# Seven half-width block products for the first feed-forward product of the last batch

## The chip, the cores and the metric

The kernel is one program on one core of a Trainium2 chip. The metric is the device time of one execution in microseconds (us), the median of a few runs. The program before has a median of 403.88 us in 3 runs (403.68 to 404.29).

## What is computed

For 8 batches of 448 tokens and 12 heads of 64 elements, attention with normalised queries and keys, and then two products with an activation between them:

```python
q_n = q / (norm(q) + 1e-06);  k_n = k / (norm(k) + 1e-06)
attn = softmax(q_n @ k_n.T / tau)            # per batch and head
x = (attn @ v), heads side by side           # 3584 x 768
h = x @ w_in                                 # 768 x 2048
g = h * clip(h + 3, 0, 6) / 6
out = g @ w_out                              # 2048 x 768
```

Inputs and output are float32 in memory; the kernel works with bf16 operands and float32 sums.

## The kernel before

The attention of a batch is six **pairs of heads**, 48 pairs in all, numbered `i`. A loop over `i` (from 18 on; the pairs before stand in a hand-written list, `PLAN`) issues one pair at a time: scores, exponentials on ACT, products with V, the loads and the normalisation for pairs to come, and between these some **units** of the two products of batches that are done. The order of each engine's queue is the order in which the program issues the work; there is no scheduler. Engines run their queues in order and wait on each other through semaphores.

A unit of the **first product** (`mm1_unit`, line 574) takes one of 16 blocks of 128 columns of `w_in` (index `fc`) over all 448 tokens of a batch. It is six matmuls with 448 moving columns, one for each block of 128 rows of `w_in`. ACT then makes `u = relu(h/6 + 1/2)` (line 589), and DVE `g = min(u, 1) * h` in bf16 (line 595). The result for the last batch goes to `g_last`, a part of the buffer `big`, whose loads have ended by then; for the others it goes to `gT0` or `gT1`.

The **second product** (`product_unit`, line 734) already works by seven block products in place of eight. Token blocks of 128 are taken in pairs (numbered 0 to 10 here), and each pair is a 2 x 2 block product in seven parts named "1" to "7". Each part is eight matmuls with 384 moving columns (line 753). "4.8" is part 4 of pair 8. Parts 3 and 4 take plain blocks, the others sums of two blocks. Those sums are made by DVE from bf16 blocks (`g_sum`, line 713, the operation at line 731), 128x1024 elements each. ACT copies some parts out (lines 772, 801), POOL adds copies in three operations (lines 782, 783, 786), and DVE adds the rest (lines 778, 810). A token block without a partner is a `single_unit` (line 824, "s6.0" for batch 6), 16 matmuls and a copy by DVE (line 843).

After the loop comes a **last stage**, `units[NP]` (lines 903 to 912): two units of the first product of batch 6, all 16 of batch 7, pairs 7 and 8 and the single block of batch 6, and then pairs 9 and 10, which need the whole first product of batch 7. Each unit's work on ACT, DVE and POOL is issued right behind its matmuls.

Results of matmuls lie in a ring of six PSUM banks (`M` x4, `Y`, `Z`), taken strictly in turn (`next_bank`). A unit cannot start before the bank's last reader is done. In the loop, POOL squares and normalises queries and keys (lines 229, 286), casts V (line 305) and copies small key blocks (line 392). These stop with pair 47, so POOL's last operation in the loop is the cast that starts at 322.59 us of the trace.

Of the kernel before, what the change touches and what calls it, by code (L numbers as in the profile page):

```python
# [8 lines left out]
FP32 = mybir.dt.float32  # L9
BF16 = mybir.dt.bfloat16  # L10
AF = mybir.ActivationFunctionType
ALU = mybir.AluOpType
# [47 lines left out]
]  # L60


@with_exitstack
def kernel(
# [10 lines left out]
    nc = tc.nc  # L75
    B, H, S, D = q.shape
    d_model, d_ff = moe_w_in.shape
    inv_tau = 1.0 / float(tau)

    HP = H // 2  # L80
    NP = B * HP
    CC = d_model // 128
    FCN = d_ff // 128
    MH = d_model // 2
    SM = 384
    SR = S - SM
# [7 lines left out]
    sb = ctx.enter_context(tc.tile_pool(name="sb", bufs=2))  # L94
# [28 lines left out]
    RAW, VAL, SUM = 14 * D, 20 * D, KC * 128 // 2  # L123
    big = const.tile([128, (NR + 2) * RAW + NV * VAL], FP32, name="big", tag="big")
# [20 lines left out]
    nrms = [const.tile([128, 7, 2, D], BF16, name=f"nrm{i}", tag=f"nrm{i}") for i in range(3)]  # L145
# [3 lines left out]
    bias = const.tile([128, 2], FP32, name="bias", tag="bias")  # L149
    eps_bias, half_bias = bias[:, 0:1], bias[:, 1:2]  # L150
# [402 lines left out]
    def g_of(b):  # L553
        if b == B - 1:
            needs(("NM", NP - 1), ("RE", NP - 1), ("VC", NP - 1))
            return g_last
        return gT[b % 2]
# [90 lines left out]
    def firsts(b, *fcs):  # L648
        return [(mm1_unit, b, fc) for fc in fcs]
# [13 lines left out]
    summed, g_summed, issued_products = set(), set(), set()  # L663
# [7 lines left out]
    wide = [big[:, c : c + MH] for c in range(0, 3 * MH, MH)]  # L671
    wide_late = [tail(c, MH) for c in range(TAIL, TAIL + 2 * (len(PAIRS) - LOOP) * MH, MH)]

    def sum_of(n, what):

        if what == "e":
            return gs["1"] if n < B - 2 else late_sums[1]["e"]
        if n < LOOP or n == len(PAIRS) - 1:
            return gs[what + str(n % 2) if what == "7" else what]
        return late_sums[n % 2][what]  # L680
# [143 lines left out]
    def single_unit(b, m):  # L824
# [21 lines left out]

        post["v"].append(store)

    def sums(n, names):
        return [(g_sum, n, x) for x in names]  # L850

# [3 lines left out]
    def products(text):  # L855

        u = []
        for x in text.split():
            name, n = x.split(".")
            if name[0] == "s":  # L860
                u.append((single_unit, int(name[1]), int(n)))
            else:
                u.append((product_unit, int(n), name[0], None, name[1:] == "a"))
        return u
# [9 lines left out]
    APART = {(n, y) for n in range(len(PAIRS)) for x, y in (("5a", "3"), ("2a", "4")) if f"{x}.{n}" in " ".join(TURNS.values()).split()}  # L874
    side = {
        18: [(weight_sums, "y4", KC // 2, KC // 2)], 19: sums(0, "62"), 20: sums(0, "1"),
        21: sums(1, "75"), 22: sums(1, "621"),
        25: sums(2, "75"), 26: sums(2, "62"), 27: sums(2, "1"), 28: [(g_left, 2)], 29: sums(2, "e"),
        31: sums(3, "75"), 32: sums(3, "62"), 33: sums(3, "1"),
        34: sums(4, "75"), 35: sums(4, "621"), 37: [(g_left, 4)],  # L880
        38: sums(5, "75"), 39: sums(5, "62"), 40: sums(5, "1"), 41: sums(4, "e"),
        43: sums(6, "75"), 44: sums(6, "62"), 45: sums(6, "1"), 46: sums(7, "75"), 47: sums(7, "62"),
    }
    units = {}
    carry = firsts(1, FCN - 2, FCN - 1)
    for b in range(2, B - 1):
        first = firsts(b, *range(FCN))
        for n, x in enumerate([0, 3, 3, 3, 3, 2]):
            i = (b + 1) * HP + n
            u = carry + [first.pop(0) for _ in range(x)]  # L890
            carry = []
            *p, last = products(TURNS[i])
            if i == NP - 1:
                p, last = [last], None
            x = 0 if n == 1 else 1 if n in (0, 5) and i > FIRST else 2
            units[i] = u[:x] + p + u[x:]
            units[i] += [last] if last else []
        carry = first
    units[FIRST] += sums(0, "75")

    b = B - 1
    f = firsts(b, *range(FCN))
    units[NP] = sums(7, "1") + carry[:1] + products("4.7") + carry[1:] + [(g_left, B - 2)] + products("2.7")
    units[NP] += products("3.8") + sums(8, "75") + products("1.7 4.8") + sums(8, "62") + products("6.7 5.8") + sums(8, "1")
    units[NP] += products("7.7") + sums(B - 2, "e")
    for n, x in enumerate("2176"):
        units[NP] += f[n : n + 1] + products(x + ".8")
    units[NP] += f[4:] + products(f"s{B - 2}.0") + sums(9, "75") + products(f"s{B - 2}.1") + sums(9, "62")
    units[NP] += products("3.9 4.9") + sums(9, "1") + products("5.9") + sums(10, "75") + products("2.9 3.10") + sums(10, "62")
    units[NP] += products("4.10 5.10") + sums(10, "1") + products("2.10 1.9 1.10")  # L910
    units[NP] += [(product_unit, n, x, 2) for n, x in ((9, "7"), (9, "6"), (10, "6"))]
# [38 lines left out]
    def finish_units(e):  # L950
        post[e].pop(0)()
# [15 lines left out]
    def do(op, *args):  # L967
        OPS[op](*args)
        key = (op,) + tuple(a for a in args if isinstance(a, int))
        if op not in ("RE", "NM", "LQ"):  # L970
            issued.add(key[:3] if op == "SC" else key)
# [40 lines left out]
    for i in range(FIRST, NP):  # L1012
        assert not stream
        stream = list(units[i])
        n_u = len(stream)
        even = i % 2 == 0

        def prepare(*what):
            for op, n, *args in what:
                if n < (NP // 2 if op in ("NO", "LV") else NP):  # L1020
                    do(op, n, *args)

        if i > FIRST:
# [12 lines left out]
        if (i - 1) % HP > 3:  # L1036
            do("XB", i - 1)
        elif even:
            do("XP", i - 2)
        if even:  # L1040
            prepare(("XD", i + 2))
        do("UU", 1)
        do("SC", i, 3)
        do("EX", i, 3)
        if not even:
            prepare(("CS", i + 1))
        prepare(("SQ", i + 5, "p", 0, 7))
        do("UU", 1)
        n = 2
        if i == FIRST:  # L1050
            do("RE", i + 4)
        if not even:
            prepare(("NO", (i + 3) // 2))
            if n_u > 3 and stream[0][0] is product_unit and units[i][1][0] is mm1_unit:
                do("UU", 1)
                n += 1
            prepare(("CK", i + 1), ("CK", i + 2))
        do("UU", n_u - n - 1)
        prepare(("NM", i + 3, "p"), ("VC", i + 2, "p"))
        if even:  # L1060
            prepare(("XD", i + 3))
        do("UU", 1)
        prepare(("RE", i + 5), ("LQ", i + 7))
        if not even:
            prepare(("LV", (i + 5) // 2))
        while post["p"]:
            finish_units("p")
        do("VA", i, 0)
# [42 lines left out]
```

## Time and profile before

| what | value |
|---|---|
| median of 3 runs | 403.88 us |
| lowest, highest | 403.68, 404.29 us |
| span of the profiled execution | 404.4 us |
| PE busy | 393.7 us, 97% |
| DVE busy | 288.7 us, 71% |
| ACT busy | 276.7 us, 68% |
| POOL busy | 236.7 us, 59% |
| granted TensorE clock | 1.000 |

The profiled execution has no time of its own beside its span, which is 0.5 us above the median of the runs. A span is counted from the first to the last instruction. In the views, `L580` is line 580 of the program before, `out<-in` names the tiles, and a timeline row has the start in us, the length in us, and `x6` when six instructions that follow each other are merged. A row of merged groups gives busy time and the mean length of one instruction in ns. An instruction's length contains its drain, so the pitch of matmuls in a stream is found from rows with many of them.

### The profile page before, as it was taken

What the parts mean: (1) busy time and instruction counts of PE and PEld (TensorE: products, weight loads), DVE (VectorE), ACT (ScalarE), POOL (GpSimd) and SP (SyncE); (2) the same over time, 40 slices, a digit from 0 to 9 for tenths busy, and PEclk for the clock granted to TensorE, in tenths of its full rate; (3) what the DMA queues carried; (4) which work ended last, traced back from release to release, by engine and by line L of the source; (5) the groups of instructions that cost most, each with busy time, mean ns of one, the idle gap of its engine ahead of it and who ended that gap; (6) DMA issues with size and microseconds to landing.
All of it is one profiled execution on the core that took longest, in us unless ns stands there. A gap on an engine that the chain in (4) does not pass through costs nothing.

```text
span 404.4 us, 9618 instructions
## 1 busy us (share of the span) xinstructions
PE 393.7 (97%) x3689; PEld 234.5 (58%) x3689; DVE 288.7 (71%) x512; ACT 276.7 (68%) x604; POOL 236.7 (59%) x232
## 2 busy tenths in 40 slices
PE   7798999999999999999999999999999999999996
PEld 5566656555665555655555556555565556555564
DVE  5898787878498777777857887587656666655663
ACT  4899989887377687687768768768758755225230
POOL 4799945862744997588486875876664600510070
PEclk9999999999999999999999999999999999999999
DMA  8899999999877748786779659986863523140134
GB/s 285 247 235 243 221 221 213 170 219 202 181 168 179 167 111 209 185 222 129 169 200 194 140 149 163 180 190 136 193 147 76 112 45 63 36 88 20 25 74 99
DMA packets 93166, 63.75 MB, mean 158 GB/s; under 512 B 56128, under 2 KB 93120, under 8 KB 93120
## 3 DMA queue, kind: packets, MB, share of 16 engines
q1 hardware_dynamic: 87408, 56.45, 61.1%
q0 software_dynamic: 5312, 6.29, 9.5%
q8 instruction: 29, 0.48, 0.6%
q10 hardware_dynamic: 400, 0.39, 0.3%
q14 instruction: 17, 0.14, 0.1%
HBM read 45.61 MB, written 11.01 MB: 140 GB/s over the span
## 4 chain that ended last, share of the span: by engine, by line
PE 88%; ACT 4%; DVE 3%; DMA 3%; SPq 1%; issue 0%; DVEq 0%; ACTq 0%
PE M L580 23%; PE M L753 16%; PE PV L475 11%; PE Y L580 6%; PE Z L580 6%; PE M L435 6%; PE Z L753 5%; PE Y L753 4%; PE M L833 3%; PE M L627 3%; ACT at L453 3%; DMA big<-in_q_dram 3%; PE Y L435 1%; PE Z L435 1%; PE Y L833 1%; PE Y L627 1%
## 5 line engine op out<-in xcount | busy, mean ns | idle before, releaser
L453 ACT ACTIVATE at<-M 128x448 bf16<-128x448 f32 x194 | 96.8, 564 | 23.2 <-PE M L435 20.7
L580 PEld LDWEIGHTS <-w_in_sb 128*128 128x128 bf16 x768 | 72.3, 98 | 63.1 <-issue 2.5
L580 PE MATMUL M<-xT,w_in_sb 128*128 128x448 bf16 x504 | 107.4, 352 | 0.1
L286 POOL TENSOR_TENSOR nrm<-big,r 128x896 bf16<-128x896 f32 (+1 forms) x47 | 78.1, 1665 | 14.8 <-issue 4.6
L229 POOL TENSOR_TENSOR big<-big 128x896 f32<-128x896 f32 (+5 forms) x45 | 68.1, 1519 | 14.8 <-DMA big<-in_k_dram 8.2
L589 ACT ACTIVATE u<-M,bias 128x448 bf16<-128x448 f32 x84 | 54.9, 655 | 26.3 <-PE M L580 26.0
L475 PEld LDWEIGHTS <-at 128*128 128x128 bf16 (+1 forms) x1536 | 54.1, 97 | 19.9 <-issue 12.1
L595 DVE SCALAR_TENSOR_TENSOR gT<-u,M 128x448 bf16<-128x448 bf16 x73 | 44.6, 617 | 29.2 <-ACT u L589 28.4
L475 PE MATMUL PV<-vx,at 128*128 128x65 bf16 (+1 forms) x1536 | 62.7, 194 | 0.0
L241 DVE TENSOR_REDUCE n<-big 128x14 f32<-128x896 f32 (+1 forms) x50 | 51.5, 1037 | 0.3 <-ACT big L227 0.2
L392 POOL COPY km<-tT 64x128 bf16<-64x128 bf16 x34 | 14.4, 424 | 61.9 <-PE M L435 25.9
L782 POOL TENSOR_TENSOR big<-big 128x384 f32<-128x384 f32 x11 | 11.8, 1077 | 54.6 <-ACT big L801 54.5
L753 PEld LDWEIGHTS <-gT 128*128 128x128 bf16 x288 | 27.8, 98 | 20.0 <-DVE gT L731 0.6
L753 PE MATMUL M<-w_out_sb,gT 128*128 128x384 bf16 x192 | 35.0, 326 | 0.1
L496 DVE TENSOR_TENSOR on<-PV,rc 128x512 bf16<-128x512 f32 x48 | 33.2, 691 | 1.7
L435 PE MATMUL M<-tT,kz 64*128 64x448 bf16 (+1 forms) x171 | 30.9, 351 | 0.5 <-ACT at L453 0.5
L453 ACT ACTIVATE at<-Y 128x448 bf16<-128x448 f32 x50 | 28.2, 564 | 4.3 <-PE Z L435 4.3
L753 PEld LDWEIGHTS <-gs 128*128 128x128 bf16 x224 | 21.5, 98 | 14.7 <-DVE gs L731 0.3
L453 ACT ACTIVATE at<-Z 128x448 bf16<-128x448 f32 x50 | 28.2, 565 | 2.6 <-PE M L435 2.6
L305 POOL CAST vx<-big 128x512 bf16<-128x512 f32 x39 | 28.2, 728 | 3.1 <-DMA big<-in_v_dram 3.0
L580 PE MATMUL Z<-xT,w_in_sb 128*128 128x448 bf16 x132 | 28.6, 353 | 0.0
L580 PE MATMUL Y<-xT,w_in_sb 128*128 128x448 bf16 x132 | 28.6, 352 | 0.0
(128 smaller groups left out, 574.7 us busy)
## 6 DMA issues: line engine op xcount, KB each, us to landing
big<-in_k_dram SPq DMA_DIRECT2D x24, 448.0 KB, 5.1
big<-in_q_dram SPq DMA_DIRECT2D x24, 448.0 KB, 4.5
out_dram<-o SPq DMA_DIRECT2D x107, 96.0 KB, 2.2
big<-in_v_dram SPq DMA_DIRECT2D x48, 128.0 KB, 4.7
big<-in_v_dram SPq DMA_DIRECT2D x48, 96.0 KB, 4.4
w_in_sb<-in_moe_w_in_dram POOLq DMA_DIRECT2D x8, 384.0 KB, 10.4
w_out_sb<-in_moe_w_out_dram POOLq DMA_DIRECT2D x4, 768.0 KB, 10.8
tT<-nrm SPq DMA_TRANSPOSE x34, 2.8
```

The costliest lines, as they stand in the source:

```text
L229: engines[e].tensor_tensor(out=o, in0=i, in1=i, op=ALU.mult)
L241: nc.vector.tensor_reduce(out=n2_and_r[0][:, d % 2, j % 2, c], in_=sq[:, :, :, :].rearrange("p g c d -> p (g c) d")[:, c, :], axis=AX.X, o ...
L286: engines[e].tensor_tensor(out=nrm[:, :, g, :].rearrange("p c g d -> p g c d"), in0=raw_of[j][:, g, :, :], in1=n2_and_r[4][:, d % 2, j % 2, :]
L305: (engines[e].copy if e == "a" else engines[e].tensor_copy)(out=o, in_=f)
L435: nc.tensor.matmul(o, ks, qt[rows], start=True, stop=True)
L453: nc.scalar.activation(out=o, in_=x, func=AF.Exp, scale=inv_tau)
L475: nc.tensor.matmul(pv_out(j, h), at[rows, n, q_cols(i // HP, j)], vt[rows, 3 + h if name == "M" else 5 * h + int(name[1]), :], start=(name ...
L496: nc.vector.tensor_tensor(out=on[:, :, :, :].rearrange("p j h d -> p h j d"), in0=pv4[:, :, :, 0:D], in1=rc[:, :, :].to_broadcast([128, 2, ...
L580: nc.tensor.matmul(ps[:, 0:S], w_in_sb[:, cc, fc * 128 : (fc + 1) * 128], x[:, cc, 0:S], start=(cc == 0), stop=(cc == CC - 1),)
L589: nc.scalar.activation(out=u[:, :], in_=ps[:, 0:S], func=AF.Relu, bias=half_bias, scale=1.0 / 6.0)
L595: nc.vector.scalar_tensor_tensor(out=g[:, fc, c0 : c0 + S], in0=u[:, :], scalar=1.0, in1=ps[:, 0:S], op0=ALU.min, op1=ALU.mult,)
L753: nc.tensor.matmul(m, lhs[:, c, :], rhs[:, c, c0 : c0 + width], start=(base is None and c == 0), stop=(c == KC - 1), skip_group_check=True,)
```

## The change

The first product of the last batch (batch 7) no longer runs as 16 units of six matmuls. It runs as **eight groups**, numbered `n` from 0 to 7. Group `n` makes columns blocks `n` and `n + 8` for both halves of the tokens (224 each): a 2 x 2 block product over the halves of the columns of `w_in`, the halves of its rows, and the halves of the tokens, in **seven** products of three matmuls with 224 moving columns. A group has four PE units: A (parts 3 and 4, sometimes 1), B (part 7, sometimes 1), C (parts 5 and 2) and D (part 6).

What comes with it:

- 20 sums of blocks of `w_in` (`w_sum_of`, 128x768 bf16), five for each two groups. 13 are issued on POOL inside the loop: one in pair 44, six in pair 45, six in pair 46. Seven are in the last stage, five on DVE and two on POOL. They are put in buffers that are free by then.
- Five sums of blocks of x (`x_sum_of`, 128x672 bf16) on DVE in the last stage.
- For each group: a copy of A's bank by ACT (128x448), for six groups one more of part 1 (128x224); one or two additions on POOL (128x224 float32); on DVE a difference (128x448, `L1014` or `L1017` of the program after, the latter with a 128x224 addition), a second addition when D is done (`L1022`), and two activation products, one from PSUM (`L973`) and one from the sum in SBUF (`L992`, for two groups on POOL instead). ACT makes two or three relus.
- The last stage up to pair 9 is a written list, `LAST`, in another order than before. From "3.9 4.9" on the list is the old one.

The core of the diff:

```diff
+LAST = [
+    "w7.3v g7:1 4.7 w7.2v f14 f15 x3 2.7 x4 g8:6 1.7 x7 4.8 x6 x1 A1 g8:2 6.7 3.8 B1 2.8 g8:7 gl A0 w1.3v",
+    "g8:5 g8:1 A3 g6:e C1 5.8 B0 D1 C0 A2 B3 w6.3p w2.2p D0 C3 s6.1 C2 B2 A4 D3 D2 1.8 w2.3v C4 B4 A5 D4",
+    "w5.3v 6.8 C5 A6 B5 A7 D5 C6 B6 C7 B7 D6 7.8 D7 7.7 g9:6 g9:7 s6.0 g9:2 g9:5",
+]
+H_BY, M1_BY = "vvpvvvpv", "pvpvpppp"
...
+    def w_sum_of(x, p, e):
...
+        engines[e].tensor_tensor(out=w_block[x, p], in0=y, in1=z, op=op)
...
+        nc.vector.tensor_tensor(out=x_block[x], in0=y, in1=z, op=op)
...
+            for c in range(KH):
+                nc.tensor.matmul(
+                    ps[:, HS * right : HS * right + HS],
+                    w[:, c, :],
+                    x[:, c, :],
...
+        def copied():
+            nc.scalar.copy(out=s, in_=seven[n]["A"][0][:, 0:S])
+            if M1_BY[n] == "p":
+                nc.scalar.copy(out=t[:, 0:HS], in_=seven[n]["B"][0][:, HS:S])
...
+                nc.gpsimd.tensor_tensor(out=t[:, HS:S], in0=s[:, 0:HS], in1=s[:, HS:S], op=ALU.add)
+                if M1_BY[n] == "p":
+                    nc.gpsimd.tensor_tensor(out=t[:, 0:HS], in0=t[:, HS:S], in1=t[:, 0:HS], op=ALU.add)
...
+        def last():
+            nc.vector.tensor_tensor(out=h, in0=ps[:, 0:S], in1=h, op=ALU.add)
...
+                if e == "v":
+                    nc.vector.scalar_tensor_tensor(out=o, in0=x, scalar=1.0, in1=y, op0=ALU.min, op1=ALU.mult)
+                else:
+                    nc.gpsimd.tensor_tensor(out=o, in0=x, in1=y, op=ALU.mult)
...
+    w_sums = [(w_sum_of, x, p) for p in range(FCN // 4) for x in "15672"]
+    late = {44: "p", 45: "pppppp", 46: "pppppp"}
...
-    b = B - 1
-    f = firsts(b, *range(FCN))
-    units[NP] = sums(7, "1") + carry[:1] + products("4.7") + carry[1:] + [(g_left, B - 2)] + products("2.7")
-    units[NP] += products("3.8") + sums(8, "75") + products("1.7 4.8") + sums(8, "62") + products("6.7 5.8") + sums(8, "1")
-    units[NP] += products("7.7") + sums(B - 2, "e")
-    for n, x in enumerate("2176"):
-        units[NP] += f[n : n + 1] + products(x + ".8")
-    units[NP] += f[4:] + products(f"s{B - 2}.0") + sums(9, "75") + products(f"s{B - 2}.1") + sums(9, "62")
+    units[NP] = [x for line in LAST for x in listed(line)]
...
         prepare(("NM", i + 3, "p"), ("VC", i + 2, "p"))
+        for e in late.get(i, ""):
+            f, *args = w_sums.pop(0)
+            f(*args, e)
```

In `LAST`, "f14" is a unit of the first product of batch 6, "x3" a sum of x blocks, "w7.3v" a sum of weights on DVE (p: on POOL), "g8:6" a sum for pair 8, "gl" a copy of a leftover block, and "A1" the unit A of group 1.

More of the change, by code (lines that the diff above doesn't have):

```diff
@@ L672, with flat, pieces @@
     wide_late = [tail(c, MH) for c in range(TAIL, TAIL + 2 * (len(PAIRS) - LOOP) * MH, MH)]
+    HS, KH, BL = S // 2, CC // 2, B - 1
+    two_wide = 2 * KH * 128
+    def flat(t):
+        return t.rearrange("p " + " ".join("abcd"[: len(t.shape) - 1]) + " -> p (" + " ".join("abcd"[: len(t.shape) - 1]) + ")")
+    def pieces(t, n):
+        return [t[:, x * n : x * n + n] for x in range(t.shape[1] // n)]
+    gaps = [flat(t[:, :, :, :])[:, 0:two_wide] for t in nrms]
+    gaps += [x.bitcast(BF16) for x in wide_late[2:]]
+    gaps += pieces(big[:, TAIL - 4 * SUM : TAIL - SUM].bitcast(BF16), two_wide)
+    gaps += [big[:, 3 * MH : 3 * MH + two_wide // 2].bitcast(BF16)]
+    gaps += [flat(t[:, :, :, :])[:, 0:two_wide] for t in tT]
+    w_block = {}
+    for p in range(FCN // 4):
+        for y, x in enumerate("15672"):
+            if p == 0:
+                rows = g_last[:, (2, 4, 6, 10, 12)[y] :][:, 0:2, SR : SR + KH * 128]
+                w_block[x, p] = rows.rearrange("p i (c n) -> p c i n", c=KH)
+            else:
+                w_block[x, p] = gaps[5 * p - 5 + y].rearrange("p (c i n) -> p c i n", c=KH, i=2)
+    x_block = {
+        x: flat(ats[2][y][:, :, :])[:, 0 : KH * HS].rearrange("p (c n) -> p c n", c=KH) for y, x in enumerate("13467")
+    }
+    spare = flat(gT[BL % 2][:, :, :]).bitcast(FP32)
+    trio = [[spare[:, c + y * S : c + y * S + S] for y in range(3)] for c in range(0, 9 * S, 3 * S)]
     def sum_of(n, what):
@@ L847, in single_unit @@
         post["v"].append(store)
+    def w_sum_of(x, p, e):
+        f = 256 * p
+        a11, a12, a21, a22 = (
+            w_in_sb[:, KH * k : KH * k + KH, c : c + 256] for c in (f, f + d_ff // 2) for k in range(2)
+        )
+        y, z, op = {
+            "1": (a11, a22, ALU.add),
+            "2": (a21, a22, ALU.add),
+            "5": (a11, a12, ALU.add),
+            "6": (a21, a11, ALU.subtract),
+            "7": (a12, a22, ALU.subtract),
+        }[x]
+        y, z = (t.rearrange("p c (i n) -> p c i n", i=2) for t in (y, z))
+        engines[e].tensor_tensor(out=w_block[x, p], in0=y, in1=z, op=op)
+        g_summed.add(("w", x, p))
@@ new lines, in x_part, with x_sum_of @@
+    def x_part(k, t):
+        return xT[BL % 2][:, KH * k : KH * k + KH, HS * t : HS * t + HS]
+    def x_sum_of(x):
+        needs(*(("CX", i) for i in range(BL * HP, NP)))
+        b11, b12, b21, b22 = (x_part(k, t) for k in range(2) for t in range(2))
+        y, z, op = {
+            "1": (b11, b22, ALU.add),
+            "3": (b12, b22, ALU.subtract),
+            "4": (b21, b11, ALU.subtract),
+            "6": (b11, b12, ALU.add),
+            "7": (b21, b22, ALU.add),
+        }[x]
+        nc.vector.tensor_tensor(out=x_block[x], in0=y, in1=z, op=op)
+        g_summed.add(("x", x))
@@ new lines, in listed @@
+    def listed(text):
+        u = []
+        for x in text.split():
+            if x == "gl":
+                u.append((g_left, B - 2))
+            elif x[0] == "g":
+                u += sums(int(x[1]), x[3:]) if x[2] == ":" else sums(int(x[1:3]), x[4:])
+            elif x[0] == "x":
+                u.append((x_sum_of, x[1]))
+            elif x[0] == "w":
+                u.append((w_sum_of, x[1], int(x[3]), x[4]))
+            elif x[0] in "ABCD":
+                u.append((seven_unit, int(x[1:]), x[0]))
+            elif x[0] in "fF":
+                u += firsts(B - 2 if x[0] == "f" else B - 1, int(x[1:]))
+            else:
+                u += products(x)
+        return u
@@ L899 @@
     units[FIRST] += sums(0, "75")
-    b = B - 1
-    f = firsts(b, *range(FCN))
-    units[NP] = sums(7, "1") + carry[:1] + products("4.7") + carry[1:] + [(g_left, B - 2)] + products("2.7")
-    units[NP] += products("3.8") + sums(8, "75") + products("1.7 4.8") + sums(8, "62") + products("6.7 5.8") + sums(8, "1")
-    units[NP] += products("7.7") + sums(B - 2, "e")
-    for n, x in enumerate("2176"):
-        units[NP] += f[n : n + 1] + products(x + ".8")
-    units[NP] += f[4:] + products(f"s{B - 2}.0") + sums(9, "75") + products(f"s{B - 2}.1") + sums(9, "62")
+    assert len(carry) == 2
+    units[NP] = [x for line in LAST for x in listed(line)]
     units[NP] += products("3.9 4.9") + sums(9, "1") + products("5.9") + sums(10, "75") + products("2.9 3.10") + sums(10, "62")
```

81 lines of the change are left out of this document (added).

## Prediction

> **What bounds the kernel now.** I read the page's engine line first, then the chain that ended last, then engine busy time by stage.
>
> ```profile
> span 404.4 us, 9618 instructions
> PE 393.7 (97%) x3689; PEld 234.5 (58%) x3689; DVE 288.7 (71%) x512; ACT 276.7 (68%) x604; POOL 236.7 (59%) x232
> PE 88%; ACT 4%; DVE 3%; DMA 3%; SPq 1%; issue 0%; DVEq 0%; ACTq 0%
> ```
>
> PE is the bound: 97% of the span busy, 88% of the chain. A stage where PE never pauses gets shorter only if PE has less to do. The busy time in stretches shows where that holds. Columns are the stretch, its length, then busy us (instructions) of PE, PEld, DVE, ACT, POOL, the granted clock, the DMA share and GB/s:
>
> ```profile
> 301.00:321.00 20.00, 20.00 (x202) 11.82 (x200) 12.05 (x21) 14.21 (x33) 9.83 (x10) 1.00 0.49 108
> 321.00:341.00 20.00, 20.00 (x199) 11.96 (x197) 12.20 (x23) 13.45 (x28) 1.23 (x3) 1.00 0.24 49
> 341.00:356.00 15.00, 15.00 (x91) 8.79 (x90) 9.97 (x17) 4.30 (x8) 5.35 (x5) 1.00 0.27 59
> 356.00:378.00 22.00, 22.00 (x123) 11.78 (x122) 10.82 (x19) 9.98 (x16) 1.00 (x1) 1.00 0.17 37
> ```
>
> The last stage starts near 341 us and has done the first product of batch 7 by 378 us. PE is busy for all 37 us of it, DVE for 10.0 + 10.8 = 20.8 us, POOL for 6.4 us. The change takes work from PE and gives work to the two engines that have room. The question is whether they still have room when each result must come in time.
>
> **PE's own saving.** These rows of the chain of waits give the start, the length and the count of matmuls that follow each other without a pause:
>
> ```profile
> 366.79 4.54 PE M L580 x24
> 386.10 7.80 PE M L753 x48
> 399.10 1.33 PE M L753 x16
> ```
>
> A matmul with 448 columns takes 4.54/24 = 0.1892 us from start to start, one with 384 takes 7.80/48 = 0.1625 us. That is 0.000417 us a column, so one with 224 takes 0.1625 - 160 x 0.000417 = 0.0958 us. The last row has 192 columns and checks the line: 1.33/16 = 0.083 measured, 0.082 by the line. Before: 16 units of six, 96 x 0.1892 = 18.16 us. After: eight groups of 21, 168 x 0.0958 = 16.09 us. **PE saves 2.07 us**, and no more is to be had: half a percent.
>
> Each matmul brings a weight load. These two rows say whether the load can hold back a short matmul:
>
> ```profile
> 334.35 0.63 PE L475 MATMUL PV<-vx,at 128*128 128x65 bf16 x16
> L580 PEld LDWEIGHTS <-w_in_sb 128*128 128x128 bf16 x768 | 72.3, 98 | 63.1 <-issue 2.5
> ```
>
> A load lasts 98 ns. If it set the pitch, the groups would take 168 x 0.098 = 16.46 us, and the saving would be 1.7 us. But 65-column matmuls with a load each start (0.63 - 0.19)/15 = 0.029 us apart, so loads overlap. I keep 2.07.
>
> **The sums of weights in the loop.** 13 sums go to POOL, of a form that the trace has not in bf16. The nearest rows:
>
> ```profile
> L229 POOL TENSOR_TENSOR big<-big 128x768 f32<-128x768 f32 x1 | 1.5, 1466 | 0.0
> L305 POOL CAST vx<-big 128x512 bf16<-128x512 f32 x39 | 28.2, 728 | 3.1 <-DMA big<-in_v_dram 3.0
> L782 POOL TENSOR_TENSOR big<-big 128x384 f32<-128x384 f32 x11 | 11.8, 1077 | 54.6 <-ACT big L801 54.5
> 322.59 0.61 POOL L305 CAST vx<-big 128x512 bf16<-128x512 f32 x1
> 344.06 0.99 POOL L782 TENSOR_TENSOR big<-big 128x384 f32<-128x384 f32 x1 [20.86 <-ACT big L801]
> ```
>
> Same size in float32: 1.47 us, and I take that. A low end is the one-input cast's rate without its waits, 0.61 x 768/512 = 0.9 us. A high end is the rate of the short additions, 1.077 x 2 = 2.15 us. POOL is idle for 20.86 us from the loop's last cast (322.59 + 0.61 = 323.2) to the first addition of pair 7. Twelve sums of 1.47 with gaps of 0.06 end at 341.6, ahead of 344.06. The thirteenth sits in pair 44, where POOL also waited. I cost them at nothing: the idle POOL hides them, and without that cover the additions of pair 7 would be late (a rival below). The DVE sums in those pairs will meet a busy POOL, but the stretch 301 to 321 already has POOL busy 9.83 of 20 us and PE still at 20.00.
>
> The Trainium skill, page "GPSIMD Engine Reference", section "Performance versus the Vector engine", gives about 2.6 cycles of 1.2 GHz an element for two inputs. By that a sum would be 1.66 us (an estimate), and twelve would end at about 343.9; the row of 1.47 us speaks for less.
>
> **DVE in the last stage.** The order of the changed program has 59 DVE instructions from the first weight sum of the stage to the last activation product of batch 7. Their prices:
>
> ```profile
> 367.54 0.62 DVE L595 SCALAR_TENSOR_TENSOR big<-u,Z 128x448 bf16<-128x448 bf16 x1 [0.56 <-ACT u L589]
> 315.72 1.14 DVE L595 SCALAR_TENSOR_TENSOR gT<-u,M 128x448 bf16<-128x448 bf16 x2
> 348.55 0.56 DVE L810 TENSOR_TENSOR big<-M,big 128x384 f32<-128x384 f32 x1
> 399.85 0.36 DVE L778 TENSOR_TENSOR o<-M,big 128x192 f32<-128x192 f32 x1
> L286 DVE TENSOR_TENSOR nrm<-big,r 128x448 bf16<-128x448 f32 x5 | 3.2, 665 | 0.0
> 345.90 0.50 DVE L571 COPY big<-gT 128x1024 bf16<-128x1024 bf16 x1
> L702 DVE TENSOR_TENSOR w_sum<-w_out_sb 128x3072 bf16<-128x3072 bf16 x2 | 3.7, 1844 | 0.0
> L731 DVE TENSOR_TENSOR gs<-gT x26: 678/681/2142, 123.5 to 342.0; 128x1024 bf16<-128x1024 bf16 x26
> ```
>
> - 32 of 448 columns (8 products from PSUM, 6 from SBUF, 8 differences, 8 second additions, 2 products of batch 6): 32 x 0.62 = 19.8 us. The six from SBUF alone may take up to the 0.665 of the nearest such row, 0.3 us more together; that stays in the range.
> - 2 of 224 columns at 0.38 (0.36 for 192): 0.8 us. 7 of 384 columns: 7 x 0.56 = 3.9 us.
> - 7 block sums at 0.68: 4.8 us. The copy: 0.5 us.
> - Bf16 sums cost 0.68 for 1024 and 1.84 for 3072 elements, so 0.54 for 768 and 0.48 for 672: 5 weight sums and 5 x sums, 5.1 us.
>
> That is **34.9 us by durations**. Two products in 1.14 us start 0.52 apart, 0.10 less than one lasts; if all could follow so closely it would be about 30.4 us. Most wait on another engine, so I take 33.5 us. Before, it was 20.8 us.
>
> PE's work in the same stage is 2 x 1.14 + 11 x 1.30 + 2.60 (the single block) + 16.09 = 35.25 us. DVE goes from 56% of the stage to about as full as PE.
>
> **What holds DVE.** DVE's block sums vary from 678 to 2142 ns. One pair of rows shows why:
>
> ```profile
> 267.41 1.69 POOL L286 TENSOR_TENSOR nrm<-big,r 128x896 bf16<-128x896 f32 x1
> 267.50 2.14 DVE L731 TENSOR_TENSOR gs<-gT 128x1024 bf16<-128x1024 bf16 x1
> L731 DVE TENSOR_TENSOR gs<-gT 128x1024 bf16<-128x1024 bf16 x26 | 25.0, 960 | 0.0
> ```
>
> The sum starts 0.09 us after a POOL operation and ends at 269.64, 0.54 us after POOL's end at 269.10: it was held until POOL let go. Over 26 such sums the mean is 960 ns against 678 undisturbed, 0.28 us lost each, with POOL busy 59% of the span. The changed stage has 24 DVE instructions whose data all come from SBUF (5 + 5 + 7 sums, 6 products, the copy), and POOL gets about 25 us of work in 37 (16 small additions at some 0.77, two products, two weight sums, the additions of pairs 7 and 8, and what is left of the loop's sums). So 24 x 0.28 = 6.7 us, between 0 and about 7.6.
>
> The Trainium skill, page "SBUF — State Buffer", section "Who interferes with whom", says that a DVE instruction with two SBUF inputs contends with a GpSimd instruction that reads SBUF, and that the second to issue is blocked until the first ends. The two rows agree, 2.14 us for 0.68. By that rule all 24 but the copy are exposed, and the products from PSUM are not.
>
> **Where lateness reaches the end.** These rows fix the ends of the stage:
>
> ```profile
> 340.81 1.30 PE L580 MATMUL M<-xT,w_in_sb 128*128 128x448 bf16 x6
> 341.99 0.68 DVE L731 TENSOR_TENSOR gs<-gT 128x1024 bf16<-128x1024 bf16 x1
> 377.04 0.63 ACT L589 ACTIVATE u<-M,bias 128x448 bf16<-128x448 f32 x1 [0.50 <-PE M L580]
> 384.64 1.46 PE L753 MATMUL Z<-w_out_sb,big 128*128 128x384 bf16 x8
> ```
>
> PE starts at 340.81 and would end D7 at 376.06. Then it has 7.7, s6.0, 3.9 and 4.9 (1.3 + 2.6 + 1.3 + 1.3 us) and starts 5.9 at 382.56. Before, that was 384.64: the 2.07 us again. 5.9 needs the sum "5" of pair 9. Behind the last product DVE does four block sums and one copy first, 4 x 0.68 + 0.56 = 3.3 us. So the last product must end by 379.2. DVE starts at 342.0 and ends it at 342.0 + 33.5 + 6.7 = 382.2: **3.0 us late** (in time with 30.4 and no holding; 4.4 late with 34.9).
>
> DVE also waits at the head of its queue: each group ends in an addition, a relu on ACT (0.63), and a product that stands one or two instructions behind that addition, while its copies, relus and POOL additions come from other queues. Banks freed late stop PE, which makes the next results late in turn. At 0 to 0.5 us for each of eight groups (0.56 is what DVE waited for one relu above), that is 0 to 4 us; I take **2.0**.
>
> Sum: -2.07 + 3.0 + 2.0 = +2.9 us on the span of 404.4, so 407.3; on the median of 403.88, **406.8 us**. Behind 5.9 nothing is changed.
>
> **The rivals.**
>
> 1. **DVE keeps up.** It stands at 30.4 us, the holding fills waits it had anyway, and 342.0 + 30.4 + 6.7 = 379.1 is just in time. Then the full saving: 401.8, or up to 403.0 with part of it lost. For it: DVE's short spacing is in the trace. Against: 24 exposed instructions. 0.20.
> 2. **Balance**: 1.3 to 2.9 us lost, within 0.2% (some 0.8 us, about what a measurement can tell from no change): 403.9. 0.10.
> 3. **POOL is the bound at the start of the stage.** The price that decides is 1.56 us a weight sum: 323.3 + 12 x 1.56 + 2.0 for DVE's holding = 344.0, when pair 7 needs POOL. At 2.15 they end at 351.1, 7 us late; about 1 us is free before 1.7 needs the result, and part of the rest overlaps with my lateness, so some 4 us more: 410.8. For it: short additions run at that rate; against: the 1.47 row. 0.10.
> 4. **The matmuls don't get shorter** because of loads: 0.4 us less saving, 407.2, inside my case.
>
> **The numbers.** My case, DVE late by 0.8 to 6 us net, has 0.60. Slower by over 0.2%: 0.60 + 0.10 = 0.70; within: 0.10; faster: 0.20. The range leaves out half of rival 1 and the far half of rival 3 with the tail of my case: 402.4 to 410.2.
>
> **What would show it.** In the changed profile: 224-column matmuls 0.096 us apart within a product; POOL weight sums near 1.47 us; DVE over 85% busy from 345 to 380 us, with instructions on SBUF data lasting up to 2 us; PE with pauses of 0.3 to 1.5 us in the last stage, and one ahead of 5.9 of about 1 us or more. I am wrong if PE stays at 100% there: then DVE has more room than its 59 instructions say. I am wrong the other way if POOL's sums run past 344 us.

## The result, and the profile after

| kernel | median of the runs | span of the profiled execution | its own time |
|---|---|---|---|
| before | 404.09 us (4 runs, 403.68 to 405.08) | 404.4 us | not given |
| after | 407.5 us (4 runs, 407.4 to 407.54) | 405.7 us | 407.52 us |

The ratio after/before is 1.0076, with a 95% interval of 1.0062 to 1.0091: slower, by about 3.1 us (0.76% of 404.09; the two medians themselves lie 3.4 us apart). The forecast was 406.8 us and slower.

The spans differ by only 1.3 us, because the two profiled executions differ in their start-up: by the loop's end the one of after is 2.15 us ahead on its own clock. So the **last stage** is compared, not the span. These rows give its two ends, first in before, then in after. The first of each pair is the last product with V of the loop, the second the matmuls that follow it, the third the last matmuls of all:

```profile
339.74 1.23 PE L475 MATMUL PV<-vx,at 128*128 128x65 bf16 x32
340.81 1.30 PE L580 MATMUL M<-xT,w_in_sb 128*128 128x448 bf16 x6
...
398.94 1.48 PE L753 MATMUL M<-w_sum,gs 128*128 128x192 bf16 x16
```

```profile
337.59 1.23 PE L482 MATMUL PV<-vx,at 128*128 128x65 bf16 x32
338.66 1.46 PE L788 MATMUL M<-w_out_sb,gT 128*128 128x384 bf16 x8
...
400.24 1.48 PE L788 MATMUL M<-w_sum,gs 128*128 128x192 bf16 x16
```

From the second row to the start of the third, and 15 matmuls of 0.0825 us more to the last one: 58.13 + 1.24 = **59.37 us before**, 61.58 + 1.24 = **62.82 us after**. Both numbers are used below as "the stage". It grew by 3.45 us. A pause of PE is the time from one matmul's start to the next, less 0.000417 us a column and 0.0025 us. Added up over the stage, before has none and after has 5.51 us: 59.37 - 2.06 + 5.51 = 62.82.

The page and the stretches of after, with the same columns as for before (the first two stretches lie in the stage, the third is the loop's end):

```profile
PE 392.2 (97%) x3761; PEld 240.9 (59%) x3761; DVE 306.0 (75%) x538; ACT 283.2 (70%) x620; POOL 275.1 (68%) x263
...
PE 83%; DVE 9%; ACT 5%; issue 2%; DVEq 0%; ACTq 0%
```

```profile
341.00:356.00 15.00, 14.19 (x99) 9.23 (x97) 13.46 (x22) 5.66 (x11) 7.59 (x9) 1.00 0.29 62
356.00:378.00 22.00, 19.85 (x175) 16.55 (x174) 17.22 (x32) 12.61 (x25) 14.14 (x16) 1.00 0.13 28
321.00:341.00 20.00, 20.00 (x199) 12.08 (x198) 15.40 (x23) 11.80 (x25) 20.00 (x13) 1.00 0.20 41
```

PE is no longer full: 14.19 of 15 and 19.85 of 22 us. DVE entered the chain (9% for 3%). But DVE is full only in the first stretch, 13.46 of 15 us. In the second, where PE loses most, DVE works 17.22 of 22 us: PE waits for DVE, and DVE waits too. The third row shows POOL without a gap at the loop's end, 20.00 of 20 us.

The pauses of PE, from the starts in the timeline of after. The last column of a row names what ended the wait:

```profile
342.23 1.46 PE L788 MATMUL M<-w_out_sb,gT 128*128 128x384 bf16 x8
343.88 1.47 PE L788 MATMUL Z<-w_sum,gs 128*128 128x384 bf16 x8 [0.19 <-DVE gs L766]
...
348.12 1.46 PE L788 MATMUL Z<-w_sum,gs 128*128 128x384 bf16 x8 [0.62 <-DVE big L845]
...
356.70 0.45 PE L947 MATMUL M<-at,big 128*128 128x224 bf16 x3 [0.35 <-DVE gT L1019]
...
359.57 0.45 PE L947 MATMUL M<-xT,big 128*128 128x224 bf16 x3
361.32 1.46 PE L868 MATMUL Y<-w_out_sb,gT 128*128 128x384 bf16 x8 [1.30 <-DVE big L973]
...
367.04 1.46 PE L788 MATMUL M<-w_sum,big 128*128 128x384 bf16 x8 [0.41 <-DVE big L973]
...
383.40 1.46 PE L788 MATMUL M<-w_out_sb,big 128*128 128x384 bf16 x8
385.93 1.47 PE L788 MATMUL Z<-w_out_sb,big 128*128 128x384 bf16 x8 [1.07 <-DVE big L766]
```

One by hand: three matmuls from 359.57 end their turn at 359.57 + 3 x 0.0958 = 359.86, and s6.1 starts at 361.32, so 1.46 us are lost there. In the same way 0.35 us are lost at 343.88 and 1.23 us at 385.93 (383.40 + 8 x 0.1625 = 384.70). There are three groups: **1.40 us early** (0.35, 0.14, 0.13 and 0.78, up to 348.12), **2.80 us in the middle** (0.51, 1.46, 0.25 and 0.58), and **1.23 us ahead of 5.9** (0.06 us stands alone).

### The profile page after: what moved, and what is told of

It reads as the page before. It is cut to its first block, busy times and chain, and to the rows that moved or that the text cites. A ratio compares the mean times of both kernels' runs of the same rounds, so it can differ in the third digit from the quotient of the medians.

```text
span 405.7 us, 9865 instructions
## 1 busy us (share of the span) xinstructions
PE 392.2 (97%) x3761; PEld 240.9 (59%) x3761; DVE 306.0 (75%) x538; ACT 283.2 (70%) x620; POOL 275.1 (68%) x263
## 4 chain that ended last, share of the span: by engine, by line
PE 83%; DVE 9%; ACT 5%; issue 2%; DVEq 0%; ACTq 0%
PE M L587 19%; PE M L788 14%; PE PV L482 10%; PE Z L587 6%; PE M L442 6%; PE Y L587 5%; PE Z L788 4%; PE Y L788 4%; PE M L634 3%; PE M L868 3%; ACT at L460 2%; PE PV L1136 2%; PE M L947 2%; PE Y L442 1%; PE Z L442 1%
## 5 line engine op out<-in xcount | busy, mean ns | idle before, releaser
L587 PEld LDWEIGHTS <-w_in_sb 128*128 128x128 bf16 x672 | 62.9, 98 | 54.8 <-issue 2.5
L587 PE MATMUL M<-xT,w_in_sb 128*128 128x448 bf16 x438 | 94.0, 352 | 0.1
L596 ACT ACTIVATE u<-M,bias 128x448 bf16<-128x448 f32 x73 | 47.8, 657 | 14.4 <-PE M L587 13.5
L788 PE MATMUL M<-w_out_sb,gT 128*128 128x384 bf16 x208 | 37.9, 326 | 0.0
L587 PE MATMUL Z<-xT,w_in_sb 128*128 128x448 bf16 x120 | 26.0, 353 | 0.0
L766 DVE TENSOR_TENSOR gs<-gT 128x1024 bf16<-128x1024 bf16 x26 | 25.5, 981 | 0.0
L587 PE MATMUL Y<-xT,w_in_sb 128*128 128x448 bf16 x114 | 24.7, 352 | 0.0
```

The source lines that it names most:

```text
L587: nc.tensor.matmul(ps[:, 0:S], w_in_sb[:, cc, fc * 128 : (fc + 1) * 128], x[:, cc, 0:S], start=(cc == 0), stop=(cc == CC - 1),)
L596: nc.scalar.activation(out=u[:, :], in_=ps[:, 0:S], func=AF.Relu, bias=half_bias, scale=1.0 / 6.0)
L788: nc.tensor.matmul(m, lhs[:, c, :], rhs[:, c, c0 : c0 + width], start=(base is None and c == 0), stop=(c == KC - 1), skip_group_check=True,)
```

## The experiments

The theory on record (the **load theory** below): PE's saving is real, and DVE is late because it has too much work beside a busy POOL. The rival that came from reading the profile after (the **queue theory**): DVE has room, but work stands in the wrong order in its queue and in ACT's. A third, the **holding theory**, makes the time that POOL holds DVE most of the loss. All ratios are to runs of before on the same chip, with 95% intervals.

| run | median us | ratio to before | stage us | pauses us |
|---|---|---|---|---|
| e1_pe_alone | 402.26 | 0.9951 [0.9929, 0.9974] | 57.31 | 0.00 |
| e2_no_loop_sums | 406.26 | 1.0053 [1.0029, 1.0077] | 61.40 | 4.09 |
| e3_no_sums | 408.35 | 1.0090 [1.0064, 1.0116] | 61.23 | 3.93 |
| e5_loop_sums_alone | 404.26 | 1.0000 [0.9979, 1.0021] | 59.37 | 0.00 |
| e7_relu_first | 405.38 | 1.0032 [1.0008, 1.0056] | 60.38 | 3.07 |
| e8_relu_sum5 | 404.98 | 1.0024 [1.0008, 1.0039] | 59.85 | 2.54 |
| e9_relu_no_loop_sums | 403.70 | 0.9989 [0.9971, 1.0006] | 58.96 | 1.65 |
| e10_list | 403.68 | 0.9983 [0.9964, 1.0003] | 58.70 | 1.39 |
| e11_list_old_relu | 407.56 | 1.0092 [1.0062, 1.0122] | 62.62 | 5.31 |
| e12_tail_order | 402.75 | 0.9964 [0.9943, 0.9985] | 57.61 | 0.30 |

### PE's saving alone

The kernel before, with the batch's 96 matmuls of 448 columns replaced by 168 of 224. Parts of the sum are left out or added twice, and the other engines' work is unchanged. The core of the edit:

```diff
+        if b == B - 1:
+            n_mm = 10 + (fc >= FCN // 2)
+            for y in range(n_mm):
+                cc, c1 = y // 2 % CC, y % 2 * (S // 2)
...
```

> The kernel before, in which the 16 units of the last batch's first product do 168 matmuls of 224 columns in place of 96 of 448 (10 or 11 a unit, parts of the sum left out or added twice), and nothing else is changed. This is the changed kernel's PE work without its additions. All theories say that PE's saving is real: 2.07 us less than before, 402.0 on a median of 404.1. If short matmuls pay for their weight loads (0.098 us each) it is 1.7 us less; if they bring nothing, no change.

Measured: the stage is 57.31 us, 2.06 us less, with PE at 22.00 of 22 us and DVE at 12.14 (the row of the stretch, then two of PE's timeline):

```profile
351.00:373.00 22.00, 22.00 (x206) 19.62 (x204) 12.14 (x20) 10.44 (x17) 1.57 (x2) 1.00 0.23 50
```

```profile
371.78 0.74 PE L583 MATMUL M<-xT,w_in_sb 128*128 128x224 bf16 x6
372.36 1.46 PE L846 MATMUL M<-w_out_sb,big 128*128 128x384 bf16 x8
```

Six matmuls of 224 columns in 372.36 - 371.78 = 0.58 us are 0.0967 each, the forecast pitch of 0.0958 within the rows' rounding. The saving exists, and weight loads do not take it back. What has to be explained is 5.5 us of pauses.

### Without the sums

In the first run the 13 sums in the loop are left out, in the second all 20 sums of weights and the five of x. The matmuls read plain blocks instead.

```diff
-            f(*args, e)
+            w_plain(*args)
```

> The changed kernel without the 13 sums of weights on POOL in the loop (plain blocks of w_in are read in their place). Holding theory (DVE waits while POOL reads SBUF, which is most of the loss): the DVE sums of pairs 46 and 47 and the first ones of the last stage are no longer held, so the stage starts some 1.4 us or more earlier on DVE and the pauses of PE at 343 to 348 us (1.4 us together) go: 405.3 to 406.1 against 407.5. Queue theory (the order of ACT's and DVE's queues makes the pauses, each difference behind a relu that stands behind another group's relu): the later pauses of 4.1 us stay, so at most 1.4 us are won, 406.1. Load theory (59 DVE instructions are too many): no gain over 0.4 us.

> The changed kernel without any of the 20 sums of w_in and the five of x. DVE has 5.1 us less to do in the last stage and POOL is free. Load theory: DVE keeps up and nearly the full saving comes, 402 to 403. Holding theory: what is left of POOL's work still holds six products and seven sums, 403.5 to 405. Queue theory: pauses from 356 us on stay, 404.5 to 406.

Without the loop's sums the 1.40 us of early pauses are gone; 0.51, 1.46 and 1.23 us stay to the hundredth. Without any sums, pauses of 0.51, 1.46, 0.65 and 1.23 us stay. If too much work on DVE were the cause, ten instructions less would have had to shorten those. So **the load theory falls** for all but the early pauses. The median of the second run lies above all that was expected of it: 408.35 us, though its trace shows the stage 1.6 us shorter than in after. In its profiled execution (407.73 us) the 1.6 us were lost at the start: the 101st matmul starts at 16.79 us, for 15.20 in after. Why its six runs, 406.16 to 409.75 us, are all that long stays open, and I read this run by its stage alone.

What the loop's sums do shows in the queues of POOL and DVE, here in after:

```profile
333.08 8.92 POOL L898 TENSOR_TENSOR big<-w_in_sb 128x768 bf16<-128x768 bf16 x5
341.96 1.31 POOL L817 TENSOR_TENSOR big<-big 128x384 f32<-128x384 f32 x1
```

```profile
334.89 1.98 DVE L766 TENSOR_TENSOR gs<-gT 128x1024 bf16<-128x1024 bf16 x1
336.90 2.01 DVE L766 TENSOR_TENSOR gT<-gT 128x1024 bf16<-128x1024 bf16 x1
...
341.20 1.22 DVE L898 TENSOR_TENSOR tT<-w_in_sb 128x768 bf16<-128x768 bf16 x1
342.34 1.48 DVE L766 TENSOR_TENSOR gs<-gT 128x1024 bf16<-128x1024 bf16 x1
343.74 1.35 DVE L898 TENSOR_TENSOR big<-w_in_sb 128x768 bf16<-128x768 bf16 x1
...
351.71 0.55 DVE L898 TENSOR_TENSOR big<-w_in_sb 128x768 bf16<-128x768 bf16 x1
```

The last row is a weight sum that meets an idle POOL: 0.55 us. The first two rows are block sums of the loop's last pair, which take 1.98 and 2.01 us for 0.68. So DVE comes to the row 341.20, its first of the stage, 2.54 us behind PE's first matmul of the stage; without the loop's sums it is 1.19 us. That row and the next two take 1.22, 1.48 and 1.35 us for 0.55, 0.68 and 0.55: 0.67 and 0.80 us more are lost beside the loop's last sum and pair 7's first addition. The product 343.88 waits for the row 342.34. The 0.80 us of the third row are lost to pair 7's additions: it takes 1.35 us without the loop's sums as well, where PE has no early pause.

### The loop's sums alone

Before, with the 13 sums on POOL in pairs 44 to 46, which nothing reads.

```diff
+        for e in late.get(i, ""):
+            f, *args = w_sums.pop(0)
+            f(*args, e)
```

> This is the kernel before with the 13 sums of weights that the kernel after places on GpSimd in pairs 44 to 46, read by nothing here. My prediction costed them at nothing in the loop and put what is left of them, some 20 us of full GpSimd at the stage's start, on the early waits. If only that start counts: the stage of before has pauses of 0.5 to 1.5 us within its first 20 us and the time rises by 0.5 to 1.5 us (404.8 to 405.8). If before's stage, which takes its pace from PE with DVE well ahead, covers it: no change within 0.3 us, 404.1 to 404.7. If the loop itself pays for DVE instructions held by GpSimd (2.01 us for a sum that takes 0.68): the pitch of pairs 45 to 47 grows and the time rises by more than 1.5 us.

```profile
321.20 6.42 POOL L885 TENSOR_TENSOR big<-w_in_sb 128x768 bf16<-128x768 bf16 x4
327.58 5.73 POOL L885 TENSOR_TENSOR nrm<-w_in_sb 128x768 bf16<-128x768 bf16 x3
333.27 8.93 POOL L885 TENSOR_TENSOR big<-w_in_sb 128x768 bf16<-128x768 bf16 x5
342.15 1.45 POOL L804 TENSOR_TENSOR big<-big 128x384 f32<-128x384 f32 x1
```

No change: ratio 1.0000, stage 59.37 us, no pause. POOL is as full as in after, and DVE comes to its first row of the stage as late, 2.54 us behind PE's first matmul. The same 13 sums cost 1.42 us in after (62.82 - 61.40) and nothing here. What differs is `LAST`. Here the sum for product 1.7 is DVE's first row and ends 3.90 us into the stage, and 1.7 starts at 6.17. In after a weight sum stands ahead of it, it ends at 5.16, and 1.7 could start at 4.87. So the price seems to belong to the loop's sums together with the new order; no run takes the two weight sums alone out of the head of DVE's queue.

### The relu's place in ACT's queue

The middle pauses. These rows of after are from DVE's and from ACT's timeline:

```profile
357.19 0.62 DVE L1022 TENSOR_TENSOR gT<-M,gT 128x448 f32<-128x448 f32 x1
359.20 0.62 DVE L1014 TENSOR_TENSOR gT<-gT,Y 128x448 f32<-128x448 f32 x1 [1.39 <-ACT u L970]
359.74 1.00 DVE L992 SCALAR_TENSOR_TENSOR big<-u,gT 128x448 bf16<-128x448 bf16 x1
360.66 0.61 DVE L973 SCALAR_TENSOR_TENSOR big<-u,Y 128x448 bf16<-128x448 bf16 x1
```

```profile
357.91 0.67 ACT L984 ACTIVATE u<-gT,bias 128x448 bf16<-128x448 f32 x1 [1.28 <-DVE gT L1022]
358.48 0.61 ACT L970 ACTIVATE u<-Y,bias 128x448 bf16<-128x448 f32 x1
```

Read them as a turn. DVE ends a group's second addition (357.19 + 0.62). ACT has waited 1.28 us for that at the head of its queue and makes that group's clipped relu (L984). Only then comes the relu of the next group's part C (L970), whose bank `Y` PE had filled by 357.73. It ends at 359.09, and DVE's difference, which reads the same bank, starts at 359.20: DVE has waited 1.39 us. The product that empties `Y` (L973) ends at 361.27, and s6.1, which needs `Y`, starts at 361.32. The experiment puts the relu of part C ahead of the clipped relu:

```diff
         if part == "C":
-            post["a"].append(relu)
+            post["a"].insert(0, relu)
```

> The changed kernel with one line moved: the relu of part C (line 970) goes ahead of the previous group's relu (line 984) in ACT's queue. No work is added or left out. Queue theory: DVE's four waits of 1.4 to 1.5 us ahead of lines 1014 and 1017 shrink to some 0.3 us, and 2.0 to 3.4 us come back: 404.1 to 405.5. Holding theory and load theory: DVE is as full and as much held as before, 407.0 to 407.8.

```profile
361.87 0.63 ACT L970 ACTIVATE u<-Y,bias 128x448 bf16<-128x448 f32 x1 [1.20 <-PE Y L947]
362.40 0.66 ACT L984 ACTIVATE u<-gT,bias 128x448 bf16<-128x448 f32 x1
```

```profile
363.62 0.45 PE L947 MATMUL M<-xT,big 128*128 128x224 bf16 x3
363.91 1.46 PE L868 MATMUL Y<-w_out_sb,gT 128*128 128x384 bf16 x8
```

Now the relu waits for PE alone, and s6.1 follows the matmuls ahead of it without a pause (363.62 + 0.287 = 363.91). The stage falls by 2.44 us to 60.38. One line takes away 2.44 of the 5.51 us, with no work less: **the queue theory holds**. Of the 2.80 us in the middle 0.99 are left (0.51 and 0.48), of the 1.23 ahead of 5.9 0.66, and the early pauses (0.35, 0.14, 0.13, 0.78) stay as they were.

### The place of one sum, and whether the causes add up

```diff
-    "... 7.8 D7 7.7 g9:6 g9:7 s6.0 g9:2 g9:5",
+    "... 7.8 D7 7.7 g9:7 g9:5 s6.0 g9:6 g9:2",
```

> This is the kernel after with the C relu ahead of the previous group's clipped relu in ScalarE's queue, and with the sum "5" of pair 9 (the DVE row on which the product 5.9 waited 1.23 us in the kernel after) moved forward in the list: 7.7 g9:7 g9:5 s6.0 g9:6 g9:2. Queue theory (what PE loses late in the stage is DVE work that comes in the wrong order, not DVE work that is too much): the pause ahead of 5.9, 0.7 to 1.2 us, goes, and the stage falls from 60.38 us (relu order alone) to 59.3 to 59.9 us; time 404.2 to 405.0. Rival, DVE is simply full there: the pause moves to the next product that reads a sum of pair 9, the stage stays at 60.2 to 60.5 and the time at 405.2 to 405.6.

The pause of 0.66 us ahead of 5.9 is gone and 0.11 us appear later; the stage falls by 0.53 us to 59.85. In e9 this edit is not in, but the loop's sums are left out (plain blocks are read, as in e2):

> This is the kernel after with the C relu ahead of the previous group's clipped relu, and without the 13 sums of weights that stand in the loop (their blocks hold what the buffers held before, so this part of the computation is left out; the other seven sums stay). If the two causes add up, the early pauses (1.4 us in the kernel after, before the first group's parts) and the pause of 1.46 us ahead of s6.1 both go: the stage falls from 62.82 us to 59.0 to 59.4 us, and the time to 403.6 to 404.4, level with the kernel before. If one pays for the other (DVE, freed early, only waits later), the stage stays at 60.0 to 60.4 us as with the relu order alone, and the time at 405.0 to 405.5.

The stage is 58.96 us, 1.42 us below e7. Taking the loop's sums out of after gave 1.42 us too. The causes add up.

### The whole computation in another order

```diff
-    "w7.3v g7:1 4.7 w7.2v f14 f15 x3 2.7 x4 g8:6 1.7 x7 4.8 x6 x1 A1 g8:2 6.7 3.8 B1 2.8 g8:7 gl A0 w1.3v",
-    "g8:5 g8:1 A3 g6:e C1 5.8 B0 D1 C0 A2 B3 w6.3p w2.2p D0 C3 s6.1 C2 B2 A4 D3 D2 1.8 w2.3v C4 B4 A5 D4",
-    "w5.3v 6.8 C5 A6 B5 A7 D5 C6 B6 C7 B7 D6 7.8 D7 7.7 g9:6 g9:7 s6.0 g9:2 g9:5",
+    "g7:1 4.7 f15 f14 g8:6 x3 x4 1.7 x7 2.7 4.8 x1 A1 g8:2 x6 6.7 3.8 g8:1 2.8 w1.3v gl B1 g8:7 A0",
+    "g8:5 g6:e C1 A3 B0 5.8 w7.2v D1 C0 A2 w7.3v B3 w6.3p w2.2p D0 C3 C2 s6.1 B2 A4 D3 D2 w2.3v 1.8",
+    "C4 B4 A5 D4 6.8 w5.3v A6 B5 C5 A7 D5 C6 B6 C7 B7 D7 D6 7.7 g9:7 g9:5 7.8 s6.0 g9:6 g9:2",
-    late = {44: "p", 45: "pppppp", 46: "pppppp"}
+    late = {44: "ppp", 45: "pppppp", 46: "pppv"}
```

`H_BY` is "vvpvpvvv" here, and the relu stands first, as in e7. These are several edits at once: 12 of the loop's sums are on POOL, earlier, and one on DVE; the weight sums in the stage move; so do parts and products. The run e11 is the same kernel with that one line put back.

> The whole computation, with the C relu ahead of the previous group's clipped relu, and another list: three weight sums go to GpSimd in pair 44 in place of one, and the last loop sum to VectorE, so that GpSimd is free 3 to 5 us earlier; the two weight sums w7.2 and w7.3 that stood first in VectorE's queue in the stage, where GpSimd held them, stand behind the parts of group 3 and 2; sum 5 of pair 9 comes second; H_BY has GpSimd for groups 2 and 4. If the pauses of the kernel after are three separate causes (loop sums 1.4 us, relu order 2.4 us, place of sum 5 0.5 us), all of them lists and none of them a lack of room on VectorE, then nearly all of the 5.5 us goes: stage 57.4 to 58.5 us against 59.37 before, time 402.5 to 403.6, faster than the kernel before. Rival, VectorE has no room for 59 instructions beside GpSimd's work: the pauses move, the stage stays at 59.4 us or above and the time at 404.2 or above.

> The kernel of the run with the other list, with one line put back: the C relu behind the previous group's clipped relu in ScalarE's queue, as in the kernel after. Queue theory: the turn of waits (second addition on VectorE, clipped relu, relu, difference on VectorE) costs its 2.4 us or more in any list, since it hangs on ScalarE's order alone: stage 60 to 61.5 us, time 405.0 to 406.5. Rival, the better list alone does it and the relu's place matters only when VectorE is behind already: stage within 0.5 us of the other run's.

The early pauses are gone, and of the middle ones 0.13 and 0.16 us are left. Which of the list's edits took the early ones away, this run does not tell. The stage is 58.70 us, 0.67 below before; the expectation had 57.4 to 58.5 (and 402.5 to 403.6 for the time), and the interval still touches 1. With the relu put back the stage is 62.62 us and the time 407.56 us: that one line is worth 3.92 us here, more than the 2.44 in after's list and more than I expected. What e10 still lost was new, 0.19 and 0.85 us behind 5.9:

```profile
382.66 5.57 PE L788 MATMUL M<-w_out_sb,big 128*128 128x384 bf16 x32
388.91 1.48 PE L788 MATMUL M<-w_out_sb,big 128*128 128x384 bf16 x8 [0.69 <-DVE big L766]
```

```profile
387.33 1.52 DVE L766 TENSOR_TENSOR big<-big 128x1024 bf16<-128x1024 bf16 x1
```

```profile
387.31 0.99 POOL L817 TENSOR_TENSOR big<-big 128x384 f32<-128x384 f32 x1 [1.17 <-ACT big L836]
```

The block sum that 2.10 needs starts 0.02 us behind a POOL addition and takes 1.52 us for 0.68. The last experiment gives PE a product whose sum is long done:

```diff
-    units[NP] += products("4.10 5.10") + sums(10, "1") + products("2.10 1.9 1.10")
+    units[NP] += products("4.10 1.9") + sums(10, "1") + products("5.10 2.10 1.10")
```

> The kernel of the run e10_list with one more line changed, behind 5.9: the products 4.10, 1.9, 5.10, 2.10, 1.10 in place of 4.10, 5.10, 2.10, 1.9, 1.10. In e10_list PE lost 0.19 us ahead of 5.10 and 0.85 us ahead of 2.10, which wait for block sums of pair 10 that GpSimd's additions of pair 9 hold (1.37 to 1.52 us for 0.68); 1.9 needs a sum that was made earlier, so it can fill that time. If so: the pauses go, the stage falls from 58.70 to 57.7 to 57.9 us and the time to 402.5 to 403.1, an interval below 1. If the sums only get later with it, or 1.9 meets a bank that is not free: the stage stays at 58.5 us or above and the time at 403.4 to 404.0.

```profile
382.25 4.06 PE L788 MATMUL M<-w_out_sb,big 128*128 128x384 bf16 x24
386.14 1.47 PE L788 MATMUL M<-w_sum,big 128*128 128x384 bf16 x8
387.44 2.76 PE L788 MATMUL M<-w_out_sb,big 128*128 128x384 bf16 x16
390.04 1.47 PE L788 MATMUL Y<-w_sum,gs 128*128 128x384 bf16 x8
```

24 matmuls take 386.14 - 382.25 = 3.89 us, 16 take 2.60: 0.162 each, no pause. The stage is 57.61 us, 0.30 above the run with PE's saving alone, and the time 402.75 us, **faster than both kernels**: 0.9964 of before, interval 0.9943 to 0.9985. It does the whole computation, with as many sums, products and additions as after. DVE is fuller than in after meanwhile (the row of after, then of this run, 343 to 378 us of each):

```profile
343.00:378.00 35.00, 32.04 (x260) 24.71 (x258) 28.68 (x51) 17.07 (x35) 19.74 (x23) 1.00 0.17 36
343.00:378.00 35.00, 35.00 (x284) 27.27 (x283) 31.06 (x56) 18.67 (x38) 20.29 (x23) 1.00 0.16 35
```

At 31.06 of 35 us, 89%, DVE keeps PE at 35.00 of 35.

## Why the prediction was right, and where its steps were not

The total came out (406.8 for 407.5; +2.9 us for +3.1 by the ratio and +3.45 in the stage), and with it the sign. The steps did not all hold, and that the total came so close is in part luck.

- **PE's saving, 2.07 us: right.** 2.06 measured with the matmuls alone. The rival by which loads set the pitch (1.7 us) is out.
- **The weight sums at 1.47 us, costed at nothing: mis-sized.** They took 1.63 to 1.64 us undisturbed, and 2.08 us where one of DVE's block sums was still running when they started. Two of the first row's three did so; the second row is one undisturbed:

```profile
327.40 5.71 POOL L898 TENSOR_TENSOR nrm<-w_in_sb 128x768 bf16<-128x768 bf16 x3
```

```profile
L898 POOL TENSOR_TENSOR tT<-w_in_sb 128x768 bf16<-128x768 bf16 x1 | 1.6, 1637 | 0.0
```

  The row I chose was a square of one float32 tensor; the sums read two bf16 tensors. The estimate of 1.66 us from the Trainium skill, page "GPSIMD Engine Reference", section "Performance versus the Vector engine", agrees with the trace better than my row. Five of the 13 took 2.08. So POOL was busy until 341.96 of after's clock, which is 344.1 on before's: the point of rival 3, 1.56 us a sum, was passed. It cost 1.42 us rather than the 4 that I gave rival 3. Pair 7's first addition did come late: its copy was done at 340.69, and it started at 341.96. But the pause of 0.78 us at 348.12 was for DVE's row L845, which had POOL's results by 345.95 and stood in DVE's queue until 347.52. What counted was that DVE was late and held at the stage's start.
- **DVE held for 6.7 us: too much.** Up to the last product the held rows of the stage add up to 4.0 us over their undisturbed lengths: 0.67 + 0.80 + 0.80 for the three above, 0.46 for three x sums in 1.79 us, 0.92 for three of the products L992 (1.00, 0.78 and 1.00 for 0.62), 0.31 for one more weight sum. The mean of 0.28 came from a loop with POOL in operations of up to 1.7 us; in the stage most take 0.65 to 1.3, which is the likely reason. That DVE instructions with two SBUF inputs are the ones held, as the Trainium skill, page "SBUF — State Buffer", section "Who interferes with whom", states, agrees with these rows. The copy, which I took to be free of it, was not always: 1.03 us at 343.94 beside a POOL addition in e5, for 0.41 in after.
- **DVE too full, 3.0 us late at 5.9: the step that failed.** I took the lateness from volume, 33.5 + 6.7 = 40.2 us of work in a row. The 59 instructions last 34.7 us without the holding, as forecast (34.9), but they followed each other as closely as rival 1 had it. From the first weight sum at 341.20 to the last product's end at 382.99 DVE works 35.0 us, 31.0 without the holding, and waits 6.8. It is busy 28.68 of 35 us, 82%, in the stretch for which I named over 85% as the sign (345 to 380 us on before's clock). It was no sign of a loss either: e12 is at 89% there and loses 0.30 us. The last product did end late, at 382.99 of after's clock, 385.1 on before's, for 382.2 forecast and 379.2 allowed. But e12 gives DVE no instruction less and has 0.30 us of pauses, so the volume was not the limit; the order was. Rival 1, "DVE keeps up", was open to this design in another order.
- **Waits at the head of DVE's queue, 2.0 us: right in kind, three times too small.** The waits from 354 us to the last product add up to 1.54 + 1.39 + 1.39 + 0.27 + 0.20 + 1.39 + 0.51 = 6.7 us. I had listed the relu and the queues it shares, but priced each group alone, at 0 to 0.5 us. The turn between ACT's clipped relu and DVE's difference ties one group to the next, and this I did not see. It was worth 2.44 us of PE's pauses.
- **A pause of about 1 us or more ahead of 5.9: right**, 1.23. About 0.6 of it went with the relu's place, the rest with the place of one sum in the list.

Of the 5.5 us, then: 1.42 the loop's sums at the stage's start, 2.44 the relu's place, 0.53 the place of sum "5", and 1.1 in small waits (0.51 at 356.70, 0.48 ahead of 1.8, 0.11) that e12's list largely avoids. Two terms erred upward and two downward, so the sum was better than its parts.

## What to carry to other kernels

When an engine that is not full makes another wait, look at the heads of the queues before counting work. Follow one turn: who waits for whom, and what stands behind the waiting instruction. An in-order queue that mixes the end of one group with the start of the next ties the groups together; putting the instruction first whose input is ready cost one line here and gave 2.4 to 3.9 us. For a price, choose the row with the same number of inputs and the same type, not the one of the same size.

## What the runs showed that was not expected

- 13 more operations on POOL, over 21 us of a full engine, cost before nothing (ratio 1.0000) and after 1.42 us. A cover that hides work is a property of what stands beside it.
- From 343 to 378 us DVE is busy 89% in e12, which has 0.30 us of pauses in the whole stage, and 82% in after, which has 5.51.
- A bf16 sum of two tensors on POOL takes 1.63 us for 128x768, longer than the 1.47 us of a float32 square of the same size.
- The profiled executions of before and after stood 2.15 us apart by the loop's end, and 2.29 us apart already at the 101st matmul (17.49 and 15.20 us), which is more than PE's saving. Over all runs here the 101st matmul starts between 14.91 and 19.42 us. Stages have to be compared from their own start.
